# Doubling the last 64 columns before a transpose, writing pairs of steps by one copy, with a newly searched order of matmul blocks

## The chip, the cores and the metric

One core of one Trainium2 chip. The metric is the device time of one execution in microseconds (us), the median of several runs on the chip; the trace and its profile are of one more execution. The experiments ran in three batches on different chips, each with the kernel before beside them; its median was 2843.8 to 2845.0 us in each. TensorE, VectorE, ScalarE and GpSimd stand as PE, DVE, ACT and POOL in the profile.

## The reference

Two layers, each a recurrent attention with 8 memory rows followed by a gated feed-forward block, over 2048 rows of 576 columns:

```python
x = x + A(layernorm(x), mem0, Wq, Wk, Wv, Wo, seg_len=32)   # 64 segments, one after the other
x = x + B(layernorm(x), w1, w3, w2)                          # silu(gate) * up, 576 -> 4608 -> 576
# and both once more, with the same weights

def A(x, mem, ...):
    for s in range(n_seg):
        h = concat([mem, x[s*32:(s+1)*32]])       # 40 rows
        q, k, v = h @ Wq, h @ Wk, h @ Wv          # 32 heads of 128
        p = softmax(mask(q k^T / sqrt(128)))
        o = (p v) @ Wo
        mem, out = o[:8], o[8:]                   # the next segment needs this one's memory
```

The chain over segments is serial. The kernel hides it by running layer 1 seven steps behind layer 0 and by putting the feed-forward blocks in between.

## The kernel before

A table of nodes (PE, ACT, DVE, POOL, DMA) with their dependencies is made, and a planner records them in order of its estimated times. The order of TensorE's blocks is not planned but given as a string, one letter per block; which of ACT and DVE takes a copy ("AD" nodes) and where each copy stands in its queue, the planner decides while it walks along the letters.

```python
KINDS = {"L0tr": "a", "L1tr": "b", "POST": "p", "Ftr": "n", "QK": "Q", "QKt": "q", "SC": "S", "TR": "T", "PV": "P",
         "WO": "O", "WOt": "o", "VX": "X", "VXt": "x", "VM": "V", "VMt": "v", "FF": "F", "FFt": "f", "W2": "W", ...}
FOUR = ("QQqqpQQqqVSSvQnQqqFTQqfPSVv...TOPoTWPOaOoobWQQqqpQQSqq...xTOPonTOPoOo")    # 224 letters, cut
ORDER = FIRST + FOUR * 11 + LAST
```

Small letters `q x v o f` are blocks that use part of the array (row or column tiles), the capital ones before them the full array (V and X are column tiles of 32). A layer norm, its transposes and the writes of the transposed rows:

```python
def ln_nodes(tag, src, xn, deps, prio, writes):
    # DVE stats -> POOL pow -> DVE norm -> PE five transposes into a bank -> ACT or DVE writes
    ...
    return [node("AD", cost, wr(b), deps=[d] + more, ...) for wr, cost, more in writes]

def ln_tr(self, xn, b):                         # 576 = 4 x 128 + 64: the fifth transpose takes columns 448..575
    for c in range(5):
        c0 = min(c * P, D - P)
        self.mm(lnps(b)[:, c, :], XN[:, xn.i, c0:c0 + P], ident, is_transpose=True)

def ht_write(self, li, g, j, b):                # once for each of four steps
    for x0, co, m in X_AT[kind, role]:          # one piece (32) or two (24 and 8)
        cp(HT[:, 0:4, co:co + m], ps[:, 0:4, x0:x0 + m])
        for r in (0, 64):                       # the last 64 columns, into both halves of the partitions
            cp(HT[r:r + 64, 4, co:co + m], ps[64:128, 4, x0:x0 + m])

def xtb_write(self, bi, b):                     # for the feed-forward block: also one copy of four chunks, two of half height
    ...
```

The first part of the memory update (`HT<-YB`, on ACT) reads the bank YB that the O and `o` blocks write:

```python
yo = node("ACT", ..., em.y_odd(t), deps=wots[3:])
ye.append(node("ACT", ..., em.y_mem(t, nxt, 0), deps=wos[3:]))     # wos: O blocks, wots: o blocks of this step
ye.append(node("DVE", ..., em.y_mem(t, nxt, 1), deps=[yo] + ye))
```

Of the kernel before, what the change touches and what calls it, by code (L numbers as in the profile page):

```python
# [13 lines left out]
P = 128  # L14
# [25 lines left out]
def role(t):  # L40

    return (t - LAG) % 2
# [121 lines left out]
def actc(*ns):  # L164

    return sum(0.067 + n * 0.000833 for n in ns)


def dve(*ns):
    return sum(0.065 + n / 960.0 for n in ns)  # L170


def dveh(*ns):

    return sum(0.065 + n / 1920.0 for n in ns)

# [5 lines left out]
def ewh(*ns):  # L182
    return (actc(*ns), dveh(*ns))
# [3 lines left out]
FIRST = (  # L187
    "amQQVqqQSQvQqqTVSvqQQXqPSTPQxqTOoqSOoPOTPOooQQqqQSQqqQSVqvTQqPQqSQqTSPOOTooPaTOPOooQQqqQQSqqQSQqqVvQTQPqqSTVPSOO"
    "TovXPoTxPOOooQQqqQQSqqQqSVQqTvSQqPQqTSPOToPOOTooPOoQQqqQSpQqqVVvvnQTFfqQqSFfPQOQqqSTFfPoSWXOTFPfoxTOoPWOoFQfqQqF"
    "QQqSqfQFfqSVvTWQFqPfaFfTOSoPQQqqFSWTOFPfoTOPfoOWoVFvQqfFQfqWSVvQFfqFTQfqWPSQQqqQSFqfTQqPWFfSOTFfoPOWToPOoOboQQqq"  # L190
    "QSqXxQQqqQSqTQSQqqVvXPSTOPoTxOoPTPOOooQQpqqQQSqqQQnqqVvSSQTFqfVvFPfQTOqPWFToSfFOfPXxOFTWofPFOoofQQqqQSXxqQWFfqVv"
    "QQTqqSFPfSFQQqfqOFSofTWPFTOfPoFTOPfWOFooQqfFQqfQWQSqVqvQFqfSTWQqFPfSVvQTaQqqWFSFfPfOToPWTOoPObOXooxQQpqqQQSqQqqV"
    "QqSTSvQPQqqOTPSnXxTOoPoTOPOooVvpQQqqQqSQQqqnQSqVvTFfPQTOFPqfSQFqfXxOWTWoSoXxFfPFTOPfoWWOFfoFQqQfqQWQqqFWSSfVvQFf"
    "qWQqFTQqfPSQWOTFqPfoSOWWTFfPoFTOPfWOooVvWQQqqFQfSqFWQqfQQSqqWTFfPQFSqQqfOTWWaFSPfVTOovWPTOoPobOoQQqqpQQSqqXVvxSQ"
    "qQTqQqSQPqnTOPSXxoTOPoWTOPoOo"
)
FOUR = (
    "QQqqpQQqqVSSvQnQqqFTQqfPSVvTFQPqfOFWOTooSfPXxWFTFfPfOOWooQQqqWFQqfSFQqfQQqqVXxvSSWWTQPqQTFPqfOFfSoWWFTOfPFOTWofP"
    "WFOfooQQqqQFfqFWWQfqVVSSvvQQqqFTWQqPfSTWQFfqFSPfOWWFfoTOPoTWPOaOoobWQQqqpQQSqqQQqqVSSXxvQqTQqPXSTOPoxTOPonTOPoOo"
)  # L200
LAST = (
    "QQpqQqqQSqnQQFqSqfVVSvvQTFPqfTOQqPWTOSoXxPoFTFfPfOOWQooFqfFQqWWQqfVXxvSWFQfqWFTSfQqQqPQFQSqqfOTFWPfSoWOTFoPfFWWT"
    "OfPFOfooWQQqqFWQQqqSfVvQWFfqQSqTWQSqPFQfqVSvOWWTFfPFofTOPoTWPOoOobQQqqpQQSqqQQSqqVTSXxXvxQPqTQqPSWOToOoPTnPOOooQ"
    "QqqQpQqqSVSvQqVvQnqTQPqSFfTQFqPfOoSOTFfPFTOofPXWOxooWQQqqVvFQfqWQSqWQFqfSFfTQqQWSqWFfPQFfqTOWWFPSofTOFfPWWOTFoof"
    "PFOoWQqfQqWFQQqSqfFQfqVSvWQqTWQqSPQFqfFfSTWOWoFPfVvTWWPOoTOPbOooQqpQQqqXxSQnQqqQFfqSFfVvSTQPqFfTQqWSFOPfoFTOPfoT"
    "OPWOFooQqfFQfqQQqqSVvQqSWTQqPQSVvqFTQPfqOOSooTFfPXxOTFPWOoofQQqqFfQQSqqWQQqqSFTfVFfvWSQqPQFfqOTSoFPfWTOoPFTOfPFO"
    "fooQQqqWQqVSVvvQqQQSTqQqQPqSqTOSPOoToPTPOOoopFfnWFfFFffFfWFWFffFfFWfFFffWFFffWFWfFfFFffWFfFfWW"
)
# [10 lines left out]
def make_nodes(em, nseg, pools, o=Opt, dma_bw=230e3, load_bw=340e3):  # L219
# [4 lines left out]
    def node(*a, **k):  # L224
        n = Node(*a, **k)
        nodes.append(n)
        return n
# [10 lines left out]
    def both(t):  # L238

        return len(layers_of(t - role(t))) == 2  # L240
# [29 lines left out]
    def ln_nodes(tag, src, xn, deps, prio, writes):  # L270

        a = node("DVE", 1.16, em.ln_stats(src, xn), deps=deps, prio=prio, acq=[] if src is xn else [xn], name=tag + "stats")
        p_ = node("POOL", 0.45, em.ln_pow(xn), deps=[a], prio=prio, name=tag + "pow")
        c = node("DVE", 0.34 if src is xn else 0.48, em.ln_norm(src, xn), deps=[p_], prio=prio, name=tag + "norm")
        b = Slot("bank", users=len(writes))
        d = node("PE", 5 * 0.056, em.ln_tr(xn, b), deps=[c], prio=prio, mode="full", acq=[b], rel=[xn], name=tag + "tr")
        return [node("AD", cost, wr(b), deps=[d] + more, prio=prio, rel=[b], name=tag + "wr") for wr, cost, more in writes]

    def ht_writes(li, g):

        out = []
        for j in range(4):
            t = 4 * g + j + LAG * li
            te = t - role(t) - R_HT
            cost = ewh(96, 32, 24, 8, 24, 8) if li and both(t) else ewh(128, 32, 32)
            out.append(((lambda j: lambda b: em.ht_write(li, g, j, b))(j), cost, reads_ht.get(te, []) + reads_ht.get(te + 1, [])))
        return out

    def ht_set(li, g, nodes_):
        for j in range(4):  # L290
            ht_ready[li, 4 * g + j + LAG * li] = nodes_[j]

# [119 lines left out]
    def job(j):  # L412
# [10 lines left out]
        prev_ff = last_up[0]  # L423
        cost = ewh(512, 128, 128)
        for (bi, g) in reversed(ents):
# [94 lines left out]
class Emitter:  # L520
# [95 lines left out]
    def load_xn(self, g, xn):  # L616
        return lambda n: self.dma(self.T.XN[:, xn.i, :], self.a.x[g * P:(g + 1) * P, :])

# [68 lines left out]
    def src_ap(self, src):  # L687
        return self.T.XN[:, src.i, :] if src.pool == "xn" else self.T.XR[:, src.i, :]

# [16 lines left out]
    def ln_norm(self, src, xn):  # L706
        def f(n):
            L = self.T.LNS[:, xn.i]
            self.v("tensor_scalar", self.T.XN[:, xn.i, :], self.src_ap(src), L[:, 12:13], L[:, 15:16],
                   op0=ALU.subtract, op1=ALU.mult)  # L710
        return f

# [3 lines left out]
    def ln_tr(self, xn, b):  # L716

        def f(n):
            for c in range(5):
                c0 = min(c * P, D - P)  # L720
                self.mm(self.lnps(b)[:, c, :], self.T.XN[:, xn.i, c0:c0 + P], self.T.ident[:], True, True, is_transpose=True)
        return f

    def ht_write(self, li, g, j, b):
        def f(n):
            ps = self.lnps(b)
            t = 4 * g + j + LAG * li
            H_ = self.ht(t)
            for x0, co, m in X_AT[self.kind(t, li), role(t)]:
                x0 += j * SEG  # L730
                self.cp(n, H_[:, 0:4, co:co + m], ps[:, 0:4, x0:x0 + m])
                for r in (0, R64):
                    self.cp(n, H_[r:r + R64, 4, co:co + m], ps[R64:P, 4, x0:x0 + m])
        return f

    def xtb_write(self, bi, b):
        def f(n):
            ps = self.lnps(b)
            dst = self.T.XTB[:, :, bi * P:(bi + 1) * P]
            self.cp(n, dst[:, 0:4, :], ps[:, 0:4, :])  # L740
            for r in (0, R64):
                self.cp(n, dst[r:r + R64, 4, :], ps[R64:P, 4, :])
        return f

# [331 lines left out]
    def fin_cast(self, xr, xn):  # L1076
        return lambda n: self.act(self.T.XN[:, xn.i, :], self.T.XR[:, xr.i, :], ACT.Copy)

    def store(self, g, xn, last):
        return lambda n: (self.dma if last else self.swdma)(self.a.out[g * P:(g + 1) * P, :], self.T.XN[:, xn.i, :])  # L1080

# [6 lines left out]
def kernel(  # L1088
# [48 lines left out]
    T.XTB = sp.tile([P, 5, 2 * P], BF, name="XTB")  # L1137
    T.XN = sp.tile([P, pools["xn"], D], BF, name="XN")
    T.LNS = sp.tile([P, pools["xn"], 16], F32, name="LNS")
# [79 lines left out]
```

## Time and profile before

| | before |
|---|---|
| median, three runs | 2843.19 us (2841.11 to 2845.37) |
| span of the profiled run | 2838.2 us |
| TensorE busy | 2741.1 us, 97% |
| VectorE, ScalarE busy | 2069.6 us (73%), 1144.9 us (40%) |
| TensorE idle by part: FIRST, FOUR x 11, LAST (to the last matmul's end) | 51.5, 29.1, 12.4 us |
| one FOUR round, mean of 11 | 165.46 us |

Read it so: TensorE sets the end (92% of the chain that ended last), and "busy" for VectorE and ScalarE only matters where TensorE waits for them. The waits are few and small, and the repeated ones come at the same letter of every round. The lines are in the prediction.

### The profile page before, as it was taken

Reading aid. Unit: us, or ns where it says so; the run is one execution under the profiler, and the core shown is the slowest. Engines: PE = TensorE matmul, PEld = TensorE weight load, DVE = VectorE, ACT = ScalarE, POOL = GpSimd, SP = SyncE. Lnnn points to the kernel's source line nnn. Section 1 sums busy time; section 2 is a strip of 40 time slices with the busy share of each in tenths; the row PEclk is TensorE's granted clock in tenths of the full one; section 3 lists DMA queues with packets and bytes.
Section 4 is the critical chain, followed back from the end, with each engine's and each line's share of the span. In section 5 each row is a group of like instructions: output and inputs, shape, how many; then the busy total and the mean of one; then the engine's idle time right before and its main releaser. Section 6 shows DMA issues by size and latency. Waiting matters only on the chain.

```text
span 2838.2 us, 136886 instructions
## 1 busy us (share of the span) xinstructions
PE 2741.1 (97%) x60909; PEld 2257.2 (80%) x60909; DVE 2069.6 (73%) x5743; ACT 1144.9 (40%) x3629; POOL 328.4 (12%) x399
## 2 busy tenths in 40 slices
PE   5999999999999999999999999999999999999998
PEld 3787878788887878888787888878788887878786
DVE  4677767777777677777767777776777777777775
ACT  1434443443434344343434434343443435343332
POOL 1111110110101011010101101010110101010110
PEclk8999999999999999999999999999999999999998
DMA  9072514234241433424243342414334242423468
GB/s 301 4 201 81 167 48 142 70 103 139 62 136 58 139 88 99 138 62 136 59 138 89 96 140 63 135 57 139 88 99 138 63 135 63 141 80 107 142 176 242
DMA packets 493425, 323.84 MB, mean 114 GB/s; under 512 B 26680, under 2 KB 488000, under 8 KB 492832
## 3 DMA queue, kind: packets, MB, share of 16 engines
q1 hardware_dynamic: 489808, 308.15, 37.4%
q8 instruction: 476, 7.80, 1.2%
q0 software_dynamic: 3024, 6.93, 0.8%
q14 instruction: 117, 0.96, 0.1%
HBM read 310.26 MB, written 2.36 MB: 110 GB/s over the span
## 4 chain that ended last, share of the span: by engine, by line
PE 92%; DVE 3%; ACT 2%; DMA 2%; issue 1%; SPq 0%; POOL 0%; DVEq 0%; ACTq 0%
PE bank L539 80%; PE YB L539 12%; ACT HT L542 1%; DVE HT L545 1%; DMA W<-in_A_Wk_dram 1%; SPq L548 0%; DMA WO<-in_A_Wo_dram 0%; DVE XN L545 0%; DVE XR L545 0%; ACT OT L542 0%; DVE HTT L545 0%; DVE PB L545 0%; DVE STAT L545 0%; DVE LNS L545 0%; DVE SME L545 0%
## 5 line engine op out<-in xcount | busy, mean ns | idle before, releaser
L539 PEld LDWEIGHTS <-W 128*128 128x128 bf16 (+1 forms) x29040 | 1228.7, 99 | 156.6 <-issue 57.4
L539 PE MATMUL bank<-HT,W 128*128 128x80 bf16 (+3 forms) x22720 | 821.3, 198 | 23.4 <-ACT HT L542 11.6
L539 PE MATMUL bank<-XTB,W 128*128 128x256 bf16 (+3 forms) x6320 | 659.3, 262 | 0.2 <-DVE HT L545 0.2
L893 POOL MEMSET PB<- 128x1024 bf16 x284 | 270.0, 951 | 2117.9 <-PE bank L539 1837.0
L542 ACT ACTIVATE QKT<-bank 128x64 bf16<-128x64 f32 (+1 forms) x1371 | 316.6, 317 | 353.1 <-PE bank L539 347.8
L539 PE MATMUL YB<-OT,WO 128*128 128x80 bf16 (+3 forms) x11360 | 434.9, 199 | 22.6 <-ACT HT L542 14.2
L539 PEld LDWEIGHTS <-WO 128*128 128x128 bf16 (+1 forms) x11400 | 390.7, 102 | 62.5 <-issue 45.8
L539 PE MATMUL bank<-WV,HT 128*32 128x512 bf16 (+1 forms) x6840 | 383.1, 384 | 7.8 <-DMA WV<-in_A_Wv_dram 7.7
L545 DVE CAST QKT<-bank 128x64 bf16<-128x64 f32 (+2 forms) x693 | 186.4, 316 | 189.5 <-PE bank L539 186.4
L539 PE MATMUL bank<-W2C,HTT 128*128 128x288 bf16 x2232 | 315.6, 289 | 0.0
L542 ACT ACTIVATE HTT<-bank 128x512 bf16<-128x512 f32 (+1 forms) x324 | 178.4, 552 | 292.5 <-PE bank L539 291.2
L545 DVE TENSOR_TENSOR PB<-SME,STAT 40x128 bf16<-40x128 f32 (+1 forms) x1004 | 283.6, 321 | 15.5 <-DVE STAT L545 0.5
L539 PEld LDWEIGHTS <-HT 128*32 128x32 bf16 (+1 forms) x6840 | 149.6, 95 | 173.3 <-issue 44.2
L545 DVE TENSOR_REDUCE STAT<-SME 104x8 f32<-104x320 f32 (+1 forms) x568 | 270.5, 476 | 17.2 <-ACT SME L542 11.7
L545 DVE SCALAR_TENSOR_TENSOR XR<-bank,XR 128x288 f32<-128x288 f32 x576 | 243.5, 449 | 29.2 <-PE bank L539 23.2
L539 PEld LDWEIGHTS <-HTT 128*128 128x128 bf16 x2304 | 211.8, 98 | 57.0 <-issue 4.1
L545 DVE SCALAR_TENSOR_TENSOR HTT<-HTT,bank 128x512 bf16<-128x512 bf16 (+1 forms) x324 | 201.1, 621 | 54.0 <-ACT HTT L542 51.9
L542 ACT ACTIVATE SME<-SME 104x320 f32<-104x320 f32 (+1 forms) x284 | 133.6, 471 | 234.5 <-DVE SME L545 233.2
L542 ACT ACTIVATE PTS<-bank 128x320 bf16<-128x320 f32 (+1 forms) x387 | 149.1, 415 | 189.0 <-PE bank L539 156.2
L545 DVE TENSOR_TENSOR HTT<-HTT,bank 128x512 bf16<-128x512 bf16 (+1 forms) x324 | 203.6, 628 | 23.9 <-PE bank L539 0.5
L542 ACT ACTIVATE V<-bank 128x512 bf16<-128x512 f32 x256 | 141.8, 596 | 179.8 <-PE bank L539 177.7
L545 DVE TENSOR_TENSOR SME<-bank,maskb 104x320 f32<-104x320 f32 (+1 forms) x284 | 134.1, 485 | 109.3 <-PE bank L539 87.3
(63 smaller groups left out, 1774.6 us busy)
## 6 DMA issues: line engine op xcount, KB each, us to landing
W<-in_B_w_dram SPq DMA_DIRECT2D x612, 256.0 KB, 3.6
W2C<-in_B_w_dram SPq DMA_DIRECT2D x306, 288.0 KB, 3.2
W<-in_B_w_dram SPq DMA_DIRECT2D x612, 32.0 KB, 3.1
W<-in_B_w_dram SPq DMA_DIRECT2D x10, 512.0 KB, 9.6
XR<-in_A_x_dram POOLq DMA_DIRECT2D x16, 288.0 KB, 3.6
WO<-in_A_Wo_dram SPq DMA_DIRECT2D x4, 1152.0 KB, 11.5
W<-in_A_Wq_dram SPq DMA_DIRECT2D x8, 512.0 KB, 7.3
W<-in_A_Wk_dram SPq DMA_DIRECT2D x8, 512.0 KB, 7.3
```

The costliest lines, as they stand in the source:

```text
L539: self.ch("PE", self.nc.tensor.matmul(out, lhsT=lhsT, rhs=rhs, start=start, stop=stop, skip_group_check=True, **k))
L542: self.ch("ACT", self.nc.scalar.activation(*a, **k))
L545: self.ch("DVE", getattr(self.nc.vector, fn_)(*a, **k))
L893: return lambda n: self.ch("POOL", self.nc.gpsimd.memset(self.T.PB[:, pb.i], 0.0))
```

## The change

Its intent: the norm's result gets its last 64 columns a second time behind it (rows of 640), so that the fifth transpose fills both halves of the partitions, and one copy of five chunks does what three did. Two steps whose HT tiles lie together are written by one or two copies with a step in the access pattern. Copies of one transpose are chained. The planner's cost of a copy has a floor of 0.19 us. And the letters are new.

```diff
-    return sum(0.067 + n * 0.000833 for n in ns)                      # actc; dve and dveh alike
+    return sum(max(0.067 + n * 0.000833, 0.19) for n in ns)
-        return [node("AD", cost, wr(b), deps=[d] + more, ...) for wr, cost, more in writes]
+        for wr, cost, more in writes:
+            out.append(node("AD", cost, wr(b), deps=[d] + more + out[-1:], ...))
     # ht_writes: one entry for each pair of steps that share a tile, not one for each step      (cut)
             self.v("tensor_scalar", self.T.XN[:, xn.i, 0:D], self.src_ap(src), L[:, 12:13], L[:, 15:16], ...)
+            self.v("tensor_copy", self.T.XN[:, xn.i, D:D + R64], self.T.XN[:, xn.i, D - R64:D])
-                c0 = min(c * P, D - P)
-                self.mm(..., self.T.XN[:, xn.i, c0:c0 + P], ...)
+                self.mm(..., self.T.XN[:, xn.i, c * P:(c + 1) * P], ...)
     # ht_write:
+            if k:                                # layer 1: 24 and 8 columns of both steps
+                cp(56, 24, 0, 40, 24)
+                cp(0, 152, 24, 8, 8)
+            else:                                # 32 columns of one step or of two
+                cp(X_AT[0, role(t)][0][1], 80, 0, 32, 32)
+    def xtb_write(self, bi, b):
+        return lambda n: self.cp(n, self.T.XTB[:, :, bi * P:(bi + 1) * P], self.lnps(b))
-FOUR = ("QQqqpQQqqVSSvQnQqqFTQq...TWPOaOoobWQQqqpQQ...xTOPonTOPoOo")
+FOUR = ("QQqqQpQSqqQQSqqVvnQTFq...PWOooWQQ...TWPObOooQQqqpQQ...xTOPoaTOPonOo")
```

FIRST and LAST are new too. The matmuls are the same ones: only their order changes.

More of the change, by code (lines that the diff above doesn't have):

```diff
@@ L164, in actc @@
 def actc(*ns):
-    return sum(0.067 + n * 0.000833 for n in ns)
+    return sum(max(0.067 + n * 0.000833, 0.19) for n in ns)
 def dve(*ns):
-    return sum(0.065 + n / 960.0 for n in ns)
+    return sum(max(0.065 + n / 960.0, 0.19) for n in ns)
 def dveh(*ns):
-    return sum(0.065 + n / 1920.0 for n in ns)
+    return sum(max(0.065 + n / 1920.0, 0.19) for n in ns)
 def ew(*ns):
@@ L187 @@
 FIRST = (
-    "amQQVqqQSQvQqqTVSvqQQXqPSTPQxqTOoqSOoPOTPOooQQqqQSQqqQSVqvTQqPQqSQqTSPOOTooPaTOPOooQQqqQQSqqQSQqqVvQTQPqqSTVPSOO"
-    "TovXPoTxPOOooQQqqQQSqqQqSVQqTvSQqPQqTSPOToPOOTooPOoQQqqQSpQqqVVvvnQTFfqQqSFfPQOQqqSTFfPoSWXOTFPfoxTOoPWOoFQfqQqF"
-    "QQqSqfQFfqSVvTWQFqPfaFfTOSoPQQqqFSWTOFPfoTOPfoOWoVFvQqfFQfqWSVvQFfqFTQfqWPSQQqqQSFqfTQqPWFfSOTFfoPOWToPOoOboQQqq"
-    "QSqXxQQqqQSqTQSQqqVvXPSTOPoTxOoPTPOOooQQpqqQQSqqQQnqqVvSSQTFqfVvFPfQTOqPWFToSfFOfPXxOFTWofPFOoofQQqqQSXxqQWFfqVv"
-    "QQTqqSFPfSFQQqfqOFSofTWPFTOfPoFTOPfWOFooQqfFQqfQWQSqVqvQFqfSTWQqFPfSVvQTaQqqWFSFfPfOToPWTOoPObOXooxQQpqqQQSqQqqV"
@@ L193 @@
-    "QqSTSvQPQqqOTPSnXxTOoPoTOPOooVvpQQqqQqSQQqqnQSqVvTFfPQTOFPqfSQFqfXxOWTWoSoXxFfPFTOPfoWWOFfoFQqQfqQWQqqFWSSfVvQFf"
-    "qWQqFTQqfPSQWOTFqPfoSOWWTFfPoFTOPfWOooVvWQQqqFQfSqFWQqfQQSqqWTFfPQFSqQqfOTWWaFSPfVTOovWPTOoPobOoQQqqpQQSqqXVvxSQ"
-    "qQTqQqSQPqnTOPSXxoTOPoWTOPoOo"
+    "maQQQqqqQVvVSQqQSvTPqqQqXTQSPTqOOoSPOoTxoPOoQQqqQSQqqQQSqqVSvQTQPqqTOSoPTPOoOTPoOoQQqqVSvQQqqQSqQTQPqqaOQTqSPoSV"
+    "vXTOPoTxPOOooQQqqQqSQqQSQqqQSVTvqQqPSTOPTOoPoTPOOooQQqqpQQqqSVVSvvQqTnQFfqQPqSQTFfqXOPoSTxFPfWFOTofPOOFooQfqQQqq"
@@ new lines @@
+    "WQFSfqFfQSVvqWTQPqFSQqfFQfqTOoSPWOaTFfPoTFPfOOooWFQfqVvQFfqQSWVvqFfTQFfqWSQQqqFQPqfSQTOPqWFSofOTFPfoOWTPoOobQQqq"
+    "QSqQQqXxSqQTqVvSQPqQTqOPSoTXxOPoTOPoOoQQpqqQQSqqQnVvqSQTFfqQFqfVSPFfvWTOFQqfFPoSfXWTOPoxTOPFOoofQQqqQQSqqXVxvSQq"
+    "FQfqWFTfSQPqQTFfqaOPSWToFPfOFTOofPWOooFQfqQqFWQfSQqqQFqfSVvFQqfVvSWTQPqQTFfqOSWFPfoTFfPOoTWPOOoobQQqqQQSqqXxQQSq"
+    "qVTSvQqpQqPXxSTPOToOPoTnPOOooQQqqQpQSqqVvQnQqqSFTQqfFPfSVTWPvFWXxQqfXxTOFSofPOFoOTWPfWOFoofQQqqFWfSWFQfqQqVSvTQW"
+    "qQFfqWQFfqQFPfqSTOWFPfoSWTOFfPFOTWWoofPFOofQQqqQQqqSVvQQqqSTWQqPQWSTOFqfVSoPvWFWfFfTOPoTWPOoOboaQQqqpQQSqqVSvQQq"
@@ L196 @@
+    "qXxTSQqPQTXPqxOTSoPOWOTooPnOo"
 )
 FOUR = (
-    "QQqqpQQqqVSSvQnQqqFTQqfPSVvTFQPqfOFWOTooSfPXxWFTFfPfOOWooQQqqWFQqfSFQqfQQqqVXxvSSWWTQPqQTFPqfOFfSoWWFTOfPFOTWofP"
-    "WFOfooQQqqQFfqFWWQfqVVSSvvQQqqFTWQqPfSTWQFfqFSPfOWWFfoTOPoTWPOaOoobWQQqqpQQSqqQQqqVSSXxvQqTQqPXSTOPoxTOPonTOPoOo"
+    "QQqqQpQSqqQQSqqVvnQTFqfPSVvTQFqPfOTFOSoofPWWOFfTFfPWOooWQQqqQFQqfqSFQqfVXxvWWFTQfqSFWQPqfSFTOWQqXxfPSFTOoofPFWWT"
+    "OfPFOWoofQQqqWQFQqqfSFQqfSQFqfVvWTQPqSWQTFqfOWWoSFPfVvTWOPoTWPObOooQQqqpQQSqqQQSqqVXSxvQqTQPqXSTOPoxTOPoaTOPonOo"
@@ L200 @@
 )
 LAST = (
-    "QQpqQqqQSqnQQFqSqfVVSvvQTFPqfTOQqPWTOSoXxPoFTFfPfOOWQooFqfFQqWWQqfVXxvSWFQfqWFTSfQqQqPQFQSqqfOTFWPfSoWOTFoPfFWWT"
-    "OfPFOfooWQQqqFWQQqqSfVvQWFfqQSqTWQSqPFQfqVSvOWWTFfPFofTOPoTWPOoOobQQqqpQQSqqQQSqqVTSXxXvxQPqTQqPSWOToOoPTnPOOooQ"
-    "QqqQpQqqSVSvQqVvQnqTQPqSFfTQFqPfOoSOTFfPFTOofPXWOxooWQQqqVvFQfqWQSqWQFqfSFfTQqQWSqWFfPQFfqTOWWFPSofTOFfPWWOTFoof"
-    "PFOoWQqfQqWFQQqSqfFQfqVSvWQqTWQqSPQFqfFfSTWOWoFPfVvTWWPOoTOPbOooQqpQQqqXxSQnQqqQFfqSFfVvSTQPqFfTQqWSFOPfoFTOPfoT"
-    "OPWOFooQqfFQfqQQqqSVvQqSWTQqPQSVvqFTQPfqOOSooTFfPXxOTFPWOoofQQqqFfQQSqqWQQqqSFTfVFfvWSQqPQFfqOTSoFPfWTOoPFTOfPFO"
@@ L207 @@
-    "fooQQqqWQqVSVvvQqQQSTqQqQPqSqTOSPOoToPTPOOoopFfnWFfFFffFfWFWFffFfFWfFFffWFFffWFWfFfFFffWFfFfWW"
+    "QQpqqQVqvSQnqQFqfSTFfPQqQFqfSTWOQqPVWOToSovFfPXxFTWfPOOWooQqFQqfFQSqWQqfVvWFQqfXSxQTqFQPfqSQqWTOWFSPfoTOFoPfWTOP"
+    "FOWQoofFqfQQqqQSqWWFQfqVSTvWFfPWQTqFSPfQQqqWWFSfFfOTVovWPOoTOPbOooQQqqQQSqqQQqqVSTQqSQqXvxSXPTWPOTxoOPTpoPOOooQQ"
+    "qqQpQSqVvqnnQqFQfqFTSSfPQQqqVWTOvPoSWFTFfPfOTOooXPWWOxoFQqQfqQqSQqVvFTQSqfQFqPfQSqWTWFfQFPfqOWOToSoWFPfFTOfPWWOF"
+    "oofQqQFfqQFqfQSqWWQFSqfFWWQqfVVQqSvvWWFfTFfPQTqOSPoTOPWOoToPWOboXxpQQqqQQqqSnQQqqFfSFQSfqVvQTFPfqTOPSoTOFPWOTofP"
@@ L208 @@
+    "FOoofVvQQqqQqSFQfqVvSQqTWQqQSqPFTQqfXOPSoTWFPxfOFOToofPWOoFQfqQFfqQWqSQqFfQVSqvTFQfqWFQqSfPQOTqoPSFfWTOoPFTOfPFO"
+    "oofWQQqqVVvvSQQqqQqSQqQQSqTqPSTFPOOTooPTOPofOopnWFfFfFfFWfFFffWFfWFfFfFWfFfFWfFfFfWFFffWFfFfWW"
 )
@@ L273, in ln_nodes, with ht_set @@
         p_ = node("POOL", 0.45, em.ln_pow(xn), deps=[a], prio=prio, name=tag + "pow")
-        c = node("DVE", 0.34 if src is xn else 0.48, em.ln_norm(src, xn), deps=[p_], prio=prio, name=tag + "norm")
+        c = node("DVE", 0.46 if src is xn else 0.66, em.ln_norm(src, xn), deps=[p_], prio=prio, name=tag + "norm")
         b = Slot("bank", users=len(writes))
         d = node("PE", 5 * 0.056, em.ln_tr(xn, b), deps=[c], prio=prio, mode="full", acq=[b], rel=[xn], name=tag + "tr")
-        return [node("AD", cost, wr(b), deps=[d] + more, prio=prio, rel=[b], name=tag + "wr") for wr, cost, more in writes]
+        out = []
+        for wr, cost, more in writes:
+            out.append(node("AD", cost, wr(b), deps=[d] + more + out[-1:], prio=prio, rel=[b], name=tag + "wr"))
+        return out
     def ht_writes(li, g):
-        out = []
+        out, at = [], {}
+        for j in range(4):
+            at.setdefault((4 * g + j - role(4 * g + j + LAG * li)), []).append(j)
+        for te, js in at.items():
+            te += LAG * li - R_HT
+            cost = ewh(240, 80) if li and both(te + R_HT) else ewh(160 * len(js))
+            out.append(((lambda js: lambda b: em.ht_write(li, g, js, b))(js), cost, reads_ht.get(te, []) + reads_ht.get(te + 1, [])))
+        return out
+    def ht_set(li, g, nodes_):
+        i = -1
         for j in range(4):
             t = 4 * g + j + LAG * li
-            te = t - role(t) - R_HT
-            cost = ewh(96, 32, 24, 8, 24, 8) if li and both(t) else ewh(128, 32, 32)
-            out.append(((lambda j: lambda b: em.ht_write(li, g, j, b))(j), cost, reads_ht.get(te, []) + reads_ht.get(te + 1, [])))
-        return out
-    def ht_set(li, g, nodes_):
-        for j in range(4):
-            ht_ready[li, 4 * g + j + LAG * li] = nodes_[j]
+            i += j == 0 or role(t) == 0
+            ht_ready[li, t] = nodes_[i]
     vx_slots, vx_nodes, vx_pe, last_v = {}, {}, [None], [None]
@@ L423, in job @@
         prev_ff = last_up[0]
-        cost = ewh(512, 128, 128)
+        cost = ewh(640)
         for (bi, g) in reversed(ents):
@@ L616, in load_xn @@
     def load_xn(self, g, xn):
-        return lambda n: self.dma(self.T.XN[:, xn.i, :], self.a.x[g * P:(g + 1) * P, :])
+        return lambda n: self.dma(self.T.XN[:, xn.i, 0:D], self.a.x[g * P:(g + 1) * P, :])
     def load_x(self, g, xr):
@@ L687, in src_ap @@
     def src_ap(self, src):
-        return self.T.XN[:, src.i, :] if src.pool == "xn" else self.T.XR[:, src.i, :]
+        return self.T.XN[:, src.i, 0:D] if src.pool == "xn" else self.T.XR[:, src.i, :]
     def ln_stats(self, src, xn):
@@ L708, in f @@
             L = self.T.LNS[:, xn.i]
-            self.v("tensor_scalar", self.T.XN[:, xn.i, :], self.src_ap(src), L[:, 12:13], L[:, 15:16],
+            self.v("tensor_scalar", self.T.XN[:, xn.i, 0:D], self.src_ap(src), L[:, 12:13], L[:, 15:16],
                    op0=ALU.subtract, op1=ALU.mult)
+            self.v("tensor_copy", self.T.XN[:, xn.i, D:D + R64], self.T.XN[:, xn.i, D - R64:D])
         return f
@@ L719, in f, with ht_write, cp @@
             for c in range(5):
-                c0 = min(c * P, D - P)
-                self.mm(self.lnps(b)[:, c, :], self.T.XN[:, xn.i, c0:c0 + P], self.T.ident[:], True, True, is_transpose=True)
+                self.mm(self.lnps(b)[:, c, :], self.T.XN[:, xn.i, c * P:(c + 1) * P], self.T.ident[:], True, True, is_transpose=True)
         return f
-    def ht_write(self, li, g, j, b):
+    def ht_write(self, li, g, js, b):
         def f(n):
             ps = self.lnps(b)
-            t = 4 * g + j + LAG * li
-            H_ = self.ht(t)
-            for x0, co, m in X_AT[self.kind(t, li), role(t)]:
-                x0 += j * SEG
-                self.cp(n, H_[:, 0:4, co:co + m], ps[:, 0:4, x0:x0 + m])
-                for r in (0, R64):
-                    self.cp(n, H_[r:r + R64, 4, co:co + m], ps[R64:P, 4, x0:x0 + m])
+            t = 4 * g + js[0] + LAG * li
+            H_, x0, k = self.ht(t), js[0] * SEG, self.kind(t, li)
+            def cp(co, gap, src, apart, m):
+                d, r = H_[:, :, co:co + m], ps[:, :, x0 + src:x0 + src + m]
+                if len(js) == 2:
+                    d, r = (bass.AP(v.tensor, v.offset, [list(x) for x in v.ap][:-1] + [[by, 2], [1, m]]) for v, by in ((d, gap), (r, apart)))
+                self.cp(n, d, r)
+            if k:
+                assert len(js) == 2
+                cp(56, 24, 0, 40, 24)
+                cp(0, 152, 24, 8, 8)
+            else:
+                cp(X_AT[0, role(t)][0][1], 80, 0, 32, 32)
         return f
     def xtb_write(self, bi, b):
-        def f(n):
-            ps = self.lnps(b)
-            dst = self.T.XTB[:, :, bi * P:(bi + 1) * P]
-            self.cp(n, dst[:, 0:4, :], ps[:, 0:4, :])
-            for r in (0, R64):
-                self.cp(n, dst[r:r + R64, 4, :], ps[R64:P, 4, :])
-        return f
+        return lambda n: self.cp(n, self.T.XTB[:, :, bi * P:(bi + 1) * P], self.lnps(b))
     def v_mm(self, t, b, strips, tail):
@@ L1076, in fin_cast @@
     def fin_cast(self, xr, xn):
-        return lambda n: self.act(self.T.XN[:, xn.i, :], self.T.XR[:, xr.i, :], ACT.Copy)
+        return lambda n: self.act(self.T.XN[:, xn.i, 0:D], self.T.XR[:, xr.i, :], ACT.Copy)
     def store(self, g, xn, last):
-        return lambda n: (self.dma if last else self.swdma)(self.a.out[g * P:(g + 1) * P, :], self.T.XN[:, xn.i, :])
+        return lambda n: (self.dma if last else self.swdma)(self.a.out[g * P:(g + 1) * P, :], self.T.XN[:, xn.i, 0:D])
 class Tiles:
@@ L1137 @@
     T.XTB = sp.tile([P, 5, 2 * P], BF, name="XTB")
-    T.XN = sp.tile([P, pools["xn"], D], BF, name="XN")
+    T.XN = sp.tile([P, pools["xn"], D + R64], BF, name="XN")
     T.LNS = sp.tile([P, pools["xn"], 16], F32, name="LNS")
```

## The prediction

Passages of it that no trace of this case shows are cut. The sum came to 2843 - 14 - 4 - 2 = 2823 us, with LAST at about 0. The fence behind the first cut shows copies in the trace of before, by form (count, busy us, mean ns).

> **What bounds the kernel now.** I read the page first: engines' busy time, then the chain that ended last.
> ```profile
> PE 2741.1 (97%) x60909; PEld 2257.2 (80%) x60909; DVE 2069.6 (73%) x5743; ACT 1144.9 (40%) x3629; POOL 328.4 (12%) x399
> ...
> PE 92%; DVE 3%; ACT 2%; DMA 2%; issue 1%; SPq 0%; POOL 0%; DVEq 0%; ACTq 0%
> ```
> TensorE is the bound: 97% busy, 92% of the chain. The change leaves its 60,909 matmuls as they are. It can only win in (a) TensorE's idle time, about 97 of 2838 us including 10 us before the first matmul, and (b) the gaps inside "busy", which depend on the order. So a gain over 2% (57 us) would need well over half of all the idle time, the start-up included.
>
> Second, where the idle time lies. The order is a string of letters, one per block of matmuls: FIRST, then FOUR eleven times, then LAST. I laid the letters along the trace's matmul starts: FOUR runs from 569.8 to 2389.9 us, 165.46 us per round on average. The view of TensorE's waits in that stretch (microseconds in total, times, longest):
> ```profile
> PE YB L539 <- ACT HT L542: 10.6, 11, 1.0
> PE bank L539 <- DVE XN L545: 7.4, 11, 0.7
> PE bank L539 <- DVE YTS L545: 4.4, 7, 0.6
> PE bank L539 <- ACT HT L542: 3.8, 11, 0.3
> PE YB L539 <- ACT OT L542: 2.7, 11, 0.2
> ```
> Five waits, 29 us in all, 2.64 us per round. FIRST has 51.5 us (10.2 before the first matmul, about 20 for weights and the first HT), LAST 12.4 us.
>
> Third, why the three largest happen: the timeline of one round, around those waits (start, duration; idle time before in brackets).
> ```profile
> 1030.60 0.69 ACT L542 ACTIVATE HT<-bank 128x128 bf16<-128x128 bf16 x3 [0.77 <-PE bank L539]
> 1031.32 0.60 DVE L545 COPY HT<-bank 128x128 bf16<-128x128 bf16 x3 [1.03 <-ACT HT L542]
> 1031.96 0.69 ACT L542 ACTIVATE HT<-bank 128x128 bf16<-128x128 bf16 x3 [0.67 <-DVE HT L545]
> 1032.67 0.22 ACT L542 ACTIVATE HT<-YB 128x64 bf16<-128x64 f32 x1
> 1032.67 0.61 DVE L545 COPY HT<-bank 128x128 bf16<-128x128 bf16 x3 [0.75 <-ACT HT L542]
> 1032.94 0.34 PE L539 MATMUL YB<-OT,WO 128*64 128x80 bf16 x8 [0.97 <-ACT HT L542]
> 1033.32 0.58 DVE L545 TENSOR_SCALAR XN<-XR,LNS 128x576 bf16<-128x576 f32 x1
> ...
> 1033.95 0.45 PE L539 MATMUL bank<-ident,XN 128*128 128x128 bf16 x5 [0.68 <-DVE XN L545]
> ...
> 1035.72 2.26 DVE L545 COPY HT<-bank 128x96 bf16<-128x96 bf16 x12 [1.43 <-ACT HT L542]
> ...
> 1038.49 0.28 DVE L545 TENSOR_TENSOR YTS<-YB,YO 64x32 bf16<-64x32 f32 x2
> ...
> 1038.83 0.45 PE L539 MATMUL bank<-ident,YTS 128*128 128x128 bf16 x5 [0.63 <-DVE YTS L545]
> ```
> The writes of transposed rows into HT already run as a chain that alternates between ScalarE and VectorE, although nothing asks for it. The memory update (HT<-YB) stands behind them on ScalarE, the norm (XN) and the YTS add behind them on VectorE, and TensorE waits for each. **The writes are not the wait; they hold up what is.**
>
> [...]
> ```profile
> L542 ACT ACTIVATE HT<-bank 64x32 bf16<-64x32 bf16 x76 | 14.6, 193 | 0.9
> L542 ACT ACTIVATE XTB<-bank 128x512 bf16<-128x512 bf16 x20 | 11.8, 590 | 4.4 <-PE bank L539 4.4
> L542 ACT ACTIVATE HT<-bank 128x128 bf16<-128x128 bf16 x38 | 10.6, 278 | 23.9 <-DVE HT L545 13.2 <-PE bank L539 10.6
> L545 DVE COPY XTB<-bank 128x512 bf16<-128x512 bf16 x12 | 5.1, 424 | 5.1 <-PE bank L539 5.1
> ```
> ScalarE: (590-278)/384 = 0.81 ns per element, the fixed part 0.17 us[...]. VectorE: a copy of 128 elements took 224 ns, of 512 took 424, so 0.52 ns per element and 0.16 fixed. [...] from a block's last matmul start to the next block's first, the median is 36 ns from full to full mode and 129 to 134 ns between full, row-tiled and column-tiled modes.[...]
>
> **The change part by part.** (1) *Copies.* Transposing the last 64 columns twice puts the fifth chunk into both halves of the partitions, so one copy of five chunks replaces one of four chunks and two half-height ones. Counts in the two built programs: bank to HT 558 before, 109 after; bank to XTB 96 to 32; added 64 copies of 64 columns in XN. Before, these took 59+49 us (HT on ScalarE, VectorE) and 23+11 us (XTB). After, at the fixed cost and slope above: 109 x about 0.28 = 31, 30 XTB on ScalarE x (0.17+640x0.81 ns = 0.69) = 21, two on VectorE 1, 64 x 0.19 = 12; 65 us in place of 141. Engines that are 73% and 40% busy do not set the end; what counts is the length of the chains. Layer 1, four steps: 4 x 6 copies, two steps on each engine, 4.7 us in the timeline; after 2 pairs x 2 copies, about 1.0 us. Layer 0: 2.6 us to about 0.9. (2) *Added on the path* from W2's last matmul to the transposes: one copy, about 0.2 us on a chain of 4.4 (the distance of 3.70 below and its wait).
>
> (3) *The new order.* I counted the mode changes in the letters: 2115 before, 2168 after; FOUR 109 and 113. Pricing every neighbouring pair of blocks with its median gap in the trace of before, and each block's own length, gives TensorE's work without waits: 3.7 us more in all, 0.3 us more per FOUR. That is a sure loss.
>
> Then the distances: how much TensorE work stands between the block that starts a chain and the one that needs its end, by the same sum. For FOUR:
> - W to the layer-1 transposes: 3.70 us before (waits 0.68), 5.49 after. The chain is 4.6 with the added copy: **no wait**, -0.68.
> - The column-tiled `o` behind another `o`: it waits for HT<-YB. Once per round before (0.97), twice after at the same distance of 32 ns. Where nothing stood ahead of it on ScalarE, in FIRST, this wait was 0.32. With shorter chains I expect 2 x 0.32: -0.33.
> - POST transposes behind YTS: VectorE was 2.26 us deep in HT copies. After, four copies at most: gone, -0.40 averaged over rounds.
> - O behind the OT copies: distance 0.39 to 0.66 us, copy 0.44: gone, -0.24.
> - Q at the start of the round: the same 134 ns, 0.34 stays.
>
> That leaves 0.64+0.34 = 0.98 of 2.64 us. Each wait also costs about 0.15 us in the modelled tail of the matmul before it: 4.6 waits become 3, -0.25. I add back 0.35 for new waits that my distances miss (VectorE takes 75 of the 109 HT copies). Per round: -1.66-0.25+0.35+0.3 = -1.26; times 11: **-14 us**.
>
> FIRST: two waits on HT writes (3.70 and 1.70 us) should shrink to about 1 together; but three W-to-transposes distances are short (2.36, 3.42, 3.26 us, about 1 us more waiting in all) and two Q blocks now follow the transposes at once (distance 36 ns, about 0.9 each, where one had 0.7). The first softmax is at 0.34 us, but the start there waits for weights anyway. Together -4 us. LAST: Q's waits of 1.8 and 1.4 fall to about 0.4 each; the last transposes stand 36 ns behind POST where they stood 2.06 us behind and waited 1.94: +2.2; mode changes +1.0. Together about 0. A remainder of -2 for shorter chains elsewhere. Sum: 2843-14-4-2 = **2823 us**, -0.7%.
>
> **Rivals.** (A) *The waits move*: the order has more mode changes, and removed waits reappear at other semaphores (the doubled `o`, short distances in FIRST and LAST). For it: both `o` places and 36 ns distances are in the order; against: distances in FOUR are longer nearly everywhere else. It gives 2835 to 2850. (B) *Everything that waits on the two engines goes*: FOUR keeps 0.5 us of waits, FIRST and LAST lose 15: about 2800. For it: nearly all the waits of FOUR sit behind HT copies; against: Q and `o` behind HT<-YB need TensorE's own result and cannot vanish. (C) *VectorE becomes the bound locally*, since most HT copies move to it and it was 73% busy: waits on SME, PB and QKT grow; against: copies fall by 76 us over both engines. It gives about 2840.
>
> **Range and chances.** The centre takes -14 in FOUR as the firm part; 0.5 us per round either way is 6 us, FIRST and LAST together 8. With B below and A above, 2803 to 2841 should hold it 8 times in 10. Over 2% faster means under 2787, below B: 0.03. Over 2% slower needs a wait of 5 us per round that no distance shows: 0.01.
>
> **What would show it.** Right: TensorE's matmul count unchanged; HT and XTB copies about 53 us busy in all; FOUR's waits near 1.3 us per round, with "YB <- ACT HT" 22 times at about 0.3 us, "bank <- DVE XN" and "bank <- DVE YTS" gone from that stretch; five-chunk copies of 0.69 us (640) on ScalarE. Wrong: YB waits still near 1 us; TensorE's spacing at mode changes other than 0.13 us; new waits on PB or QKT in FOUR; a round that is not shorter than 165.46 us, or shorter by more than 2.5.

## The result, and the profile after

| | before | after |
|---|---|---|
| median, four runs each | 2844.28 us | 2808.33 us (2807.63 to 2813.95) |
| span of the profiled run | 2838.2 us | 2806.6 us |
| FIRST (to the first FOUR) | 569.8 us | 561.3 us |
| FOUR x 11 | 1820.1 us | 1795.3 us |
| one FOUR round | 165.26 (seven), 165.77 to 165.92 (four) | 163.19 to 163.36 |
| LAST (to the last matmul's end) | 444.2 us | 445.8 us |

The ratio is 0.9879, with a 95% interval of 0.9862 to 0.9896. A ratio here is the mean time of one kernel's runs over that of the other's in the same rounds, so not quite the ratio of the medians quoted. The kernel is 1.2% faster: inside the range predicted, and 15 us below the centre.

The page of the kernel after, engines and chain; to be read against the first lines of the prediction:

```profile
PE 2736.9 (98%) x60909; PEld 2254.4 (80%) x60909; DVE 2073.5 (74%) x5622; ACT 1074.7 (38%) x3301; POOL 327.4 (12%) x399
...
PE 94%; issue 1%; DVE 1%; ACT 1%; POOL 0%; DVEq 0%; POOLq 0%; ACTq 0%
```

The same 60,909 matmuls. ScalarE lost 70 us, VectorE gained 4, although it has 121 instructions fewer. TensorE's waits in the eleven rounds of the kernel after (561.3 to 2356.6 us; total, times, longest):

```profile
PE YB L546 <- ACT HT L549: 7.0, 22, 0.3
PE bank L546 <- ACT HT L549: 3.8, 11, 0.3
```

Of five waits two are left, at the predicted counts and sizes: the `o` wait 22 times at 0.32, the Q wait 11 times at 0.34. In place of 29.1 us the rounds hold 10.7.

The copies after, by form (count, busy us, mean ns):

```profile
L549 ACT ACTIVATE XTB<-bank 128x640 bf16<-128x640 bf16 x30 | 21.0, 701 | 9.7 <-PE bank L546 9.7
L552 DVE COPY XN<-XN 128x64 bf16<-128x64 bf16 x64 | 11.6, 181 | 2.2
L552 DVE COPY HT<-bank 128x240 bf16<-128x240 bf16 x25 | 7.0, 278 | 3.5 <-PE bank L546 2.5 <-ACT HT L549 0.9
L552 DVE COPY HT<-bank 128x160 bf16<-128x160 bf16 x22 | 5.3, 241 | 6.4 <-PE bank L546 5.3
```

A five-chunk copy on ScalarE takes 0.70 us where four chunks and two halves took 0.59 and twice 0.27; the copy that doubles the columns 0.18. For its 640 elements the prediction's 0.17 us plus 0.81 ns per element gave 0.69. The two five-chunk copies on VectorE took 0.46 us each, less than the 0.49 of a line through the 224 ns for 128 and 424 for 512.

The place of the prediction's third view, in a round of the kernel after:

```profile
1019.57 0.45 PE L546 MATMUL bank<-ident,XN 128*128 128x128 bf16 x5
1019.85 1.57 PE L546 MATMUL YB<-OT,WO 128*128 128x80 bf16 x40
1020.12 0.69 DVE L552 COPY HT<-bank 128x240 bf16<-128x240 bf16 x4 [0.22 <-PE bank L546]
1021.46 0.22 ACT L549 ACTIVATE HT<-YB 128x64 bf16<-128x64 f32 x1 [0.73 <-PE YB L546]
1021.74 0.33 PE L546 MATMUL YB<-OT,WO 128*64 128x80 bf16 x8 [0.32 <-ACT HT L549]
1024.80 0.45 PE L546 MATMUL bank<-ident,YTS 128*128 128x128 bf16 x5
```

All of layer 1's HT rows are written in 0.69 us, not 4.7 over two engines; the layer-1 transposes (1019.57) and those of YTS (1024.80) have no idle time before them. The memory update starts as soon as its matmuls are done, and the `o` behind them waits 0.32.

**Two things that only the traces of both kernels show.** First, the clock. The trace records the granted TensorE clock, 1.00 or 0.50, in stretches that are multiples of 3.41 us. In the rounds of before, four such stretches are at 0.50 (from 1199.8, 1530.9, 1862.0 and 2193.1 us), in those of after none. In each of the two traces all edges of the stretches lie whole multiples of 3.41 us apart (the four starts 97 such windows from one to the next); the other windows below are counted back on that grid. The view by windows of the kernel before (length, TensorE busy and its matmuls, clock, DMA):

```profile
1032.54:1035.95 3.41, 2.33 (x38) 1.00 0.00 0
1196.38:1199.79 3.41, 1.77 (x41) 1.00 0.00 0
1199.79:1203.20 3.41, 3.41 (x39) 0.50 0.33 94
```

The two large waits of a round lie 1 us apart. Where a window's edge falls between them (1032.54) a window has 2.33 us of work; where both fall into one (1196.38) it has 1.77, and the next is at half the clock. The W and Q blocks there took 1.64 and 2.10 us, against 1.11 and 1.14 in the rounds at full clock. The slower work also hid the YTS wait (0.63) of that round, so such a round is only 0.5 to 0.7 us longer than the others: this is why the YTS wait stands 7 times and not 11 in the prediction's second view. All four halvings in the rounds of before follow a window with 1.77 or 1.78 us of work. But the recorded busy time alone does not decide it: another window of before with 1.77 us (from 701.45) was followed by full clock, as was one with 1.48 (from 537.60), and one with 2.27 (from 52.91) was followed by half. These traces give no threshold.

Second, why VectorE did not get cheaper. Two things used up what the shorter rows of copies saved (HT and XTB: 41 us on VectorE). With the new letters the planner moved copies of V and OT from ScalarE to VectorE, 31 us more there; before, then after:

```profile
L545 DVE CAST OT<-bank 128x320 bf16<-128x320 f32 x152 | 74.1, 488 | 30.8 <-PE bank L539 27.9 <-ACT HTT L542 0.3
L545 DVE CAST V<-bank 128x512 bf16<-128x512 f32 x86 | 58.2, 678 | 48.1 <-PE bank L539 47.3
```

```profile
L552 DVE CAST OT<-bank 128x320 bf16<-128x320 f32 x181 | 86.8, 485 | 52.9 <-PE bank L546 50.1
L552 DVE CAST V<-bank 128x512 bf16<-128x512 f32 x111 | 74.6, 680 | 38.4 <-PE bank L546 38.0
```

And XN takes 24 us more: the 64 doubling copies 11.6, slower norms 12. The norms on VectorE, min/median/max ns; first the kernel after, then the same kernel with the letters of before (experiment 1):

```profile
L552 DVE TENSOR_SCALAR XN<-XN,LNS x16: 424/1030/1031, 9.7 to 2254.0; 128x576 bf16<-128x576 bf16 x16
```

```profile
L552 DVE TENSOR_SCALAR XN<-XN,LNS x16: 421/429/431, 9.7 to 2221.0; 128x576 bf16<-128x576 bf16 x16
```

In the new letters 23 of the 64 norms fall beside a GpSimd memset of PB, and take 1.03 and 1.09 us (medians of the two forms) in place of 0.43 and 0.58. No norm without a memset beside it was slow in either kernel (none over 0.58 us), and the one norm of before that has a memset beside it took 1.11. It stayed hidden in the rounds: none of the transposes there waits.

### The profile page after: what moved, and what is told of

Read it like the earlier page. It is cut to its first block, busy times and chain, and to the rows that moved or that the text cites. A ratio compares the mean times of both kernels' runs of the same rounds, so it can differ in the third digit from the quotient of the medians.

```text
span 2806.6 us, 136217 instructions
## 1 busy us (share of the span) xinstructions
PE 2736.9 (98%) x60909; PEld 2254.4 (80%) x60909; DVE 2073.5 (74%) x5622; ACT 1074.7 (38%) x3301; POOL 327.4 (12%) x399
## 4 chain that ended last, share of the span: by engine, by line
PE 94%; issue 1%; DVE 1%; ACT 1%; POOL 0%; DVEq 0%; POOLq 0%; ACTq 0%
PE bank L546 81%; PE YB L546 13%; ACT HT L549 0%; DVE PB L552 0%; DVE STAT L552 0%; DVE LNS L552 0%; DVE XR L552 0%; ACT OT L549 0%; DVE PTS L552 0%; DVE HTT L552 0%; ACT PTS L549 0%; DVE XN L552 0%; DVE HT L552 0%; POOL LNS L710 0%; DVE SME L552 0%
## 5 line engine op out<-in xcount | busy, mean ns | idle before, releaser
L549 ACT ACTIVATE QKT<-bank 128x256 bf16<-128x256 f32 (+1 forms) x1373 | 321.0, 315 | 500.1 <-PE bank L546 498.2
L552 DVE CAST QKT<-bank 128x256 bf16<-128x256 f32 (+2 forms) x691 | 184.9, 317 | 206.2 <-PE bank L546 203.9
L549 ACT ACTIVATE V<-bank 128x512 bf16<-128x512 f32 x231 | 130.4, 598 | 189.5 <-PE bank L546 189.1
```

The costliest lines, as they stand in the source:

```text
L549: self.ch("ACT", self.nc.scalar.activation(*a, **k))
L552: self.ch("DVE", getattr(self.nc.vector, fn_)(*a, **k))
```

## The experiments

The change has two halves, copies and letters, and the prediction gave each a part of the gain. The theory from the trace (A): the short copies free the queues of ACT and DVE, and the letters add little. The rival (B): the searched order pays. Then (C) is on what halves the clock and (D) on the `o` wait. Every kernel gave a correct result; each had four runs, in three rounds beside before. Medians; "round" is the usual length of a FOUR round in the trace.

| kernel | copies | letters | us | ratio to before | round | waits in FOUR |
|---|---|---|---|---|---|---|
| before | old | old | 2844 | 1 | 165.26 | 29.1 |
| after | five chunks, pairs | new | 2808.33 | 0.9879 | 163.20 | 10.7 |
| copies_only | five chunks, pairs | old | 2795.70 | 0.9835 | 162.60 | 10.4 |
| order_only | old | new | 2902.41 | 1.0212 | 170.5 | 55.5 |
| no_pairs | five chunks, single steps | old | 2789.88 | 0.9812 | 162.09 | 6.6 |
| no_pairs_new | five chunks, single steps | new | 2809.06 | 0.9873 | 163.09 | 11.2 |
| xtb_only | five chunks in XTB alone | old | 2844.16 | 1.0000 | 165.43 | 34.8 |

**1 and 2. One half each.** `copies_only` is the kernel after with the three strings of before; `order_only` is the kernel before with the three strings of after.

```diff
 # copies_only, against after                     # order_only, against before
-FIRST, FOUR, LAST = (strings of after)           -FIRST, FOUR, LAST = (strings of before)
+FIRST, FOUR, LAST = (strings of before)          +FIRST, FOUR, LAST = (strings of after)
```

> The changed kernel (doubled columns, five-chunk copies, pair copies in a chain) with the letters of the kernel before. Theory A (the short chains free the queues): in a FOUR round the wait of `o` falls from 0.97 to 0.32 us, that of the YTS transposes from 0.63 to 0, that of the layer-1 transposes from 0.68 to about 0.2 (one more copy in their chain), O and Q stay at 0.24 and 0.34; the halved clock in five of eleven rounds is gone; a round takes about 163.3 us, the kernel about 2815. Theory B (the searched order is what pays): rounds stay near 165 us, the kernel near 2838.

> The kernel before with the new letters and its old small copies. Theory A: the layer-1 transposes no longer wait, but `o` and the YTS transposes still stand behind long rows of HT copies; a FOUR round takes 164.5 to 165.5 us, the kernel 2830 to 2845. Theory B: the waits are gone with the distances, a round takes about 163.3, the kernel about 2812.

Theory A holds, and further than it said: the copies alone are 12.6 us faster than copies and letters together (intervals 0.9820 to 0.9849 against 0.9862 to 0.9896), and the letters alone make the kernel 2.1% slower. Both times missed what I expected, by 19 us below and by 57 above. For `copies_only` some 8 us of the miss are in FOUR (0.7 per round) and the rest outside, FIRST alone being 12.3 us shorter than before; for `order_only` I had named the waits, not the clock. The waits of `copies_only` in its rounds:

```profile
PE bank L546 <- ACT HT L549: 3.8, 11, 0.3
PE YB L546 <- ACT HT L549: 3.5, 11, 0.3
PE YB L546 <- ACT OT L549: 2.8, 11, 0.3
```

The waits of the layer-1 and YTS transposes are gone at the old distances, so the new distances were not needed for them. The letters took the O wait away (0.26) and added one more `o` wait (0.32) and the mode changes. The waits of `order_only` in its rounds:

```profile
PE YB L539 <- ACT HT L542: 31.3, 22, 2.5
PE bank L539 <- DVE PTS L545: 14.1, 11, 1.4
```

With the long rows of HT copies in the same places, the memory update waits on ScalarE for up to 2.5 us and the PTS copies on VectorE for 1.26. And 21 windows of these rounds, 71.7 us, ran at half the clock: the rounds with two of them took 170.5 us, the first round, with one, 169.0. So such a window costs about 1.5 us here, and most of the loss beyond the waits is the clock. The new letters lose with both kinds of copies, but far more with the old ones (58 us, against 13).

**3. What halves the clock.** The kernel before with the layer-1 transposes behind the next W.

```diff
-FOUR: ...TWPOaOoobWQQ...
+FOUR: ...TWPOaOooWbQQ...
```

> The kernel before with one pair of letters exchanged in FOUR: the layer-1 transposes come behind the next W, 1.1 us later. Theory C (the clock halves because two waits, 0.97 and 0.68 us, fall into one window of 3.41 us in five of the eleven rounds): no clock of 0.5 between 570 and 2390 us any more, the transposes no longer wait, all rounds alike at 164.4 to 164.6 us, the kernel about 11 us faster, 2832. Rival (the halved clock has another cause, of that phase of the program): the clock still halves in about five rounds.

(The trace has four slow rounds, not five.) The clock part of C is right: no half-clock window is left between 572 and 2389 us, and all eleven rounds are alike. The time part is wrong: 2840.96 us, ratio 0.9991 (0.9976 to 1.0006). The rounds of `b_after_w` took 165.25, because the transposes' wait moved to the Q blocks that need their result:

```profile
PE bank L539 <- ACT HT L542: 14.5, 23, 0.9
PE bank L539 <- DVE HT L545: 6.2, 11, 0.6
```

The wait that I took away was replaced by another further down the same chain: transposes, HT copies, Q. With the old rows of copies the chain is too long for both places of its transposes that were tried; others were not. The total of the waits grew (33.6 us against 29.1) and yet the half clock went: so here the half clock went with two of them close together, not with their sum.

**4. The `o` wait.** The kernel after with two exchanges, so that a block stands between the last O of a step and its `o` blocks.

```diff
-FOUR: ...fPWOooWQQ...  ...TWPObOooQQ...
+FOUR: ...fPWOWooQQ...  ...TWPOObooQQ...
```

> The changed kernel with two exchanges in FOUR: a W block, and the layer-1 transposes, stand between the last O of a step and the two `o` blocks behind it. Theory: the second `o` waits for the memory update (HT<-YB) only because nothing stands between; its 22 waits of 0.32 us go to 0 (behind W) and about 0.1 (behind the transposes); with 0.15 us of tail each about 0.8 us per round, 9 us in all, about 2799. Rival: the wait only moves, to Q or to the banks, and the time stays at 2808.

2799.63 us, ratio 0.9846: as expected. All 22 `o` waits are gone, nothing came in their place, and a round takes 162.38 us. A block behind the last O is enough to hide the update.

**5 and 6. Which part of the copies.** `no_pairs`: copies_only with each step written by itself. `xtb_only`: before with the doubled columns, but HT written as before.

```diff
 # no_pairs, against copies_only: one entry of ht_writes for each step, and
-                cp(56, 24, 0, 40, 24)
-                cp(0, 152, 24, 8, 8)
+            for src, co, m in X_AT[k, role(t)]:
+                cp(co, 0, src, 0, m)
 # xtb_only, against before: columns doubled and transposed as in after,
+        return lambda n: self.cp(n, self.T.XTB[:, :, bi * P:(bi + 1) * P], self.lnps(b))
```

> The new copies of five chunks with the old letters, but every step written by itself, no pairs (layer 1: 4 x 2 copies, about 2.0 us of chain in place of 4.7 before and about 1.0 with pairs). Theory A1 (halving the rows of copies is enough, pairs add little): rounds of 162.6 to 163.0 us, the kernel 2796 to 2803. Rival A2 (the pairs are the point): rounds of 163.5 or more, the kernel over 2808.

> The kernel before, its letters and its HT writes, with the columns doubled and only XTB written by one copy of five chunks. Theory A says that HT's rows of copies are what holds the queues: the waits behind HT stay (0.97, 0.68 to 0.9 with the added copy, 0.63), rounds 165 to 165.9, the kernel 2840 to 2850. Rival: the five-chunk XTB copies free ScalarE as well, the kernel below 2830.

`xtb_only` changes nothing (0.9984 to 1.0017): the XTB copies were on no wait that counts. `no_pairs` keeps the whole gain, and is a little faster than pairs (0.9798 to 0.9827 against 0.9820 to 0.9849, in different batches; the two just overlap). Its rounds have only two waits:

```profile
PE bank L545 <- ACT HT L548: 3.8, 11, 0.3
PE YB L545 <- ACT OT L548: 2.8, 11, 0.3
```

The difference in FOUR is 1789.2 less 1783.0, 6.2 us, and the eleven `o` waits of 0.32 with their tails (about 0.15 each) make 5. In the built program of `no_pairs` that `o` has no wait for `HT<-YB`; in that of `copies_only` it has (the update is recorded between two `o` blocks in 20 places, in `no_pairs` in 9). The letters and the data are the same: the planner put the update behind `o` in one and before it in the other. So the third part, pairs, adds nothing here.

**7 and 8. Can the planner be told?** `late_copies` and `late_after`: copies_only and after with one hint, so that the update is recorded behind the `o` blocks.

```diff
-                      acq=[y] if g == 0 else [], name="WO")
+                      acq=[y] if g == 0 else [], name="WO", lat=0.6 if g == NG - 1 else None)
```

> The new copies with pairs and the old letters; the planner alone is told that the last O of a step is read 0.6 us later in place of 0.22, so that the memory update is recorded after the `o` blocks and they no longer wait for it. Theory D (single-step copies were faster than pairs only because the planner then recorded the update after `o`): the 11 `o` waits of FOUR go, rounds of 162.1 us, the kernel about 2790, as with single steps. Rival (single steps are better in themselves): 2795 as with pairs.

> The changed kernel (pairs, new letters) with the same hint to the planner. By the built program one `o` wait goes and the other becomes a Q wait of the same length. Theory D: about 0.5 us per round less, rounds of 162.7, the kernel about 2803. Rival: no change, 2808.

`late_copies` took 2802.24 us, 6.5 more than without the hint, but in another batch: the intervals overlap (0.9833 to 0.9863), and FOUR is only 1.4 us longer (1790.6 against 1789.2). No gain is what it shows. The `o` waits did go, as D says, but the hint also moved the updates that had been hidden: 22 Q waits, 10.7 us, where there were 11, 3.8 us. `late_after`: 2805.08 us (0.9850 to 0.9883), rounds of 162.82, near what was expected, though again by other Q waits. So the order in which the update and `o` are recorded decides who waits, and a hint for all steps is no gain. That single steps gained by this alone is likely from the built programs, but `late_copies` moved too much to show it by itself.

**9. The other corner.** `no_pairs_new`: after with each step written by itself (the edit of `no_pairs`).

> The changed kernel with its new letters, every step written by itself. Completes the square of pairs and letters. Theory D: what counts is where the update is recorded; one of the two `o` waits is left in the built program, a Q wait comes for the other: rounds 163 to 163.4, the kernel 2803 to 2812. Rival (the new letters were searched for pairs and need them): over 2815.

2809.06 us, ratio 0.9873: no different from after. With either form of the copies, the new letters cost 13 to 19 us against the old ones.

**10 to 12. A faster kernel.** The old letters with one or two exchanges in FOUR: `best_n_mid` and `best_n_end` on copies_only, `single_n_end` on no_pairs.

```diff
-FOUR: ...TWPOaOoobWQQ...  ...xTOPonTOPoOo     # copies_only
+FOUR: ...TWPOOaoobWQQ...  ...xTOPoTOPonOo     # best_n_mid
+FOUR: ...TWPOOaoobWQQ...  ...xTOPoTOPoOno     # best_n_end
+FOUR: ...TWPOaOoobWQQ...  ...xTOPoTOPoOno     # single_n_end
```

> The new copies with the old letters, FOUR changed in two places: the layer-0 transposes now stand between the last O and its `o` blocks, and the n transposes between the last P and O. Theory: the `o` wait (0.32) and the O wait (0.26) go, with 0.15 of tail each 0.9 us per round: rounds of 161.8, the kernel about 2787. Rival: the waits move on, about 2796.

> As the one before, but the n transposes stand between the last O and the last `o`, so that Q at the start of a round finds the memory update done: `o` wait (0.32) and Q wait (0.34) go, the O wait (0.26) stays: rounds of 161.65, the kernel about 2785. Rival: the `o` behind n waits in Q's place, about 2790.

> The fastest so far (single steps, old letters) with the n transposes between the last O and the last `o` of FOUR: the Q wait of 0.34 us at the start of a round goes, with its tail 0.5 us per round: rounds of 161.6, the kernel about 2785. Rival: as before, 2790, since the wait moves to `o`.

2790.95, 2790.32 and 2790.04 us (ratios 0.9818, 0.9813, 0.9806). The aimed-at waits went (4.3, 4.2 and 3.5 us are left in FOUR), rounds took 161.93, 161.92 and 161.82 us, and FOUR 1781.7, 1781.8 and 1780.1 us. Against `no_pairs` (1783.0) that is 1 to 3 us, and the start and end, which differ by as much from run to run of the same letters, hide it. No version is clearly the best of these four; all are 1.8 to 1.9% faster than before (three of the four intervals reach past 2%) and 18 us faster than after.

## Why the prediction was right or wrong

The range held the time and the kind of change was right, but the split between the halves was wrong, and two errors in the sum (tails and letters) cancelled in part. FOUR, per round, by the prediction's own terms:

| term, us per round | predicted | measured |
|---|---|---|
| waits: from 2.64 to 0.98 | -1.66 | -1.66 |
| tails of those waits | -0.25 | about -0.57 (the rest of the sum) |
| mode changes of the new letters | +0.30 | +0.54 (TensorE's busy time, after less `copies_only`) |
| new waits that the distances miss | +0.35 | 0 |
| half clock in four rounds | not in the sum | 4 x 1.53 / 11 = -0.56 |
| sum | -1.26 | -2.25 |

- **The waits**: right to a hundredth, both in which remain and in their sizes. The wait of an undisturbed `o` had been read from FIRST of the trace before (0.32), where nothing stood ahead of it on ScalarE, and that was the right place to read it.
- **The failed term: "Pricing every neighbouring pair of blocks ... and each block's own length, gives TensorE's work without waits".** In four rounds of before, W and Q ran at half the clock, 1.53 us more, and I counted that as work which the new letters inherit. It followed two waits close together and went when these shrank (and in `b_after_w`, when they were moved apart). The page's clock row shows only tenths over 71 us, so it looked like 0.9 nearly everywhere; the clock by windows would have shown it.
- **The add-back of 0.35 us** for unseen waits was caution; none came. With the clock it makes -0.91 of the -0.99 us per round that I missed, 11 us in all.
- **"Each wait also costs about 0.15 us" and "+0.3"** were both too small and cancelled, which is luck. The 0.15 was an estimate: in the trace of before, the matmul before a repeated wait of FOUR is recorded with 198 to 202 ns, and where a block behind such a matmul does not wait, its first one starts mostly 36 to 134 ns after that matmul's start: 0.06 to 0.17 us less. The 0.15 holds for `o` (`w_b_behind_o`: 22 waits and 3.0 us of busy time less, 0.14 each), not for the transposes: the three blocks around a YTS wait took 0.99 us more than in the rounds without it, 0.36 beyond the wait of 0.63. Between `copies_only` and after, with three waits each and no half clock in their rounds, the new letters cost 0.54 us of busy time per round; how much of it is mode changes was not separated. Behind blocks of 80 columns the trace of before has 128 to 135 ns from a block's last start to the next block's first at a change of mode (118 behind S, column tiles of 40 columns, to row tiles), against 36 from full to full; with 2115 changes that is some 200 us of 2838, an estimate by the difference.
- **"W to the layer-1 transposes ... 5.49 after ... no wait", and "distance 0.39 to 0.66"**: I gave the distances the credit for two waits. `copies_only` has the first gone at 3.70 us, since the chain of 4.4 us that I had read off included the time behind HT copies. Only the O wait needed the letters.
- **"That is a sure loss"** on the mode changes was right in sign, and the doubled `o` was seen; but I added both to the copies' gain without asking what the copies would do alone. A sum for the old letters might not have shown the loss: even later I expected 163.3 us per round for `copies_only`, where after has 163.2. Only the run (162.6) showed it.
- **FIRST, LAST, remainder**: predicted -4, 0 and -2, measured -8.5, +1.6 and nothing left over. FIRST's terms as written (5.4 to 1, +1, and 2 x 0.9 for 0.7) sum to -2.3, not -4. The two long HT waits fell to 0.32 together; one of the three short W distances waited, 0.53, and the two Q waits were 0.48 and 0.74. In LAST Q's two waits went, and the last transposes waited 3.38 us against 1.94, +1.4 where I had +2.2. Two further waits there (1.7 and 3.5 us) have no releaser in the profile; before has two like them.
- **The prediction's rivals** (not the theories A to D of the experiments): (C), a VectorE that becomes the bound, did not happen. (A), waits that move, is true of the letters alone (`order_only`) and of `b_after_w`. (B) put its bet on all waits behind the two engines; `w_b_behind_o` shows that `o`'s wait, which I had said could not vanish, can.

What stays open: why the new letters lose 3.8 us in FIRST and 3.2 in LAST against the old ones with the same copies (561.3 against 557.5, 445.8 against 442.6 us); single traces, in which starts of the same letters differ by up to 6 us. In FIRST the traces point to the clock: TensorE is idle for 42.6 us in both, but busy at half clock for 24.3 us in after and 17.3 in `copies_only`; by an estimate from these, half of the 7 us more is 3.5 of the 3.8. In LAST 1.2 us are idle time; the rest is open. The floor in the planner's costs and the chaining of copies were not tested by themselves.

## What to carry to other kernels

Where one engine is nearly always busy, look at what stands ahead of a late instruction on its producer's engine: here rows of small copies that TensorE did not wait for at that point held up three results that TensorE did wait for (0.97, 0.68 and 0.63 us). When a change couples new code with a newly searched order, run the four combinations: the code was worth 1.7%, the order cost 0.4% with it and 2.1% without it. And read the granted clock window by window: in four of eleven rounds here two waits close together, 1.65 us, were followed by a window at half the clock, which cost 1.53 us more.
